# A decode block with attention and a channel MLP: the first load in two transfers, one group's query weights moved, rows of x and biases in nine transfers

## The chip, the cores and the metric

The kernel runs on one core of a Trainium2 chip. The metric is the device time of one execution in microseconds, as the median of three runs. A profiled execution gives a trace: what each engine did and when, what it waited for, and what the 16 DMA engines of the core moved. The engines are TensorE (PE, with its weight loads as PEld), VectorE (DVE), ScalarE (ACT), GpSimd (POOL) and SyncE (SP), which here only issues transfers.

## What is computed

One decode step for 4 tokens of width 448: a layer norm, attention over the last 1024 positions of a cache with 8 groups of 2 query heads of width 256, a residual, then two layer norms and an MLP of width 1792 with a second residual. All is in float32.

```
W = min(4096, max(256, Sk // 4))                      # 1024
q = (x @ wq).reshape(B, Sq, Hq, Dh).transpose(0, 2, 1, 3)
k = jnp.repeat(k_cache[:, :, Sk - W:, :], rep, axis=1)
v = jnp.repeat(v_cache[:, :, Sk - W:, :], rep, axis=1)
p = _softmax(jnp.einsum("bhqd,bhkd->bhqk", q, k) * Dh ** -0.5)
o = jnp.einsum("bhqk,bhkd->bhqd", p, v)               # then reshaped, @ wo
...
h = x + _A_ref(_layernorm(x), A_k_cache, A_v_cache, A_wq, A_wo)
y = _layernorm(_layernorm(h))
h2 = h + (_gelu(y @ w1 + b1) @ w2 + b2)
```

## The kernel before

Every weight and every key and value is used once, so the kernel is a stream of loads into SBUF with work behind it. The host packs the arrays so that one transfer brings what is used next, 128 rows (partitions) at a time.

**Loads.** The tile pool `ring` has three slots of 15872 columns. A load fills a slot whole or in part: `t0` (query weights and x of group 0, keys of group 0, most of the query weights of group 1), then `ta`, `tb`, `tc`, `td` for groups 0 to 2 and again for groups 3 to 5, then three slots `te` with the keys, values and output weights of the last groups and the two MLP matrices w1 and w2. SP issues all of these in the order of the program on one queue. From the fourth load on it waits until the slot's previous content has been read. `load` (L51 on, its transfers at L57) issues one transfer, or several of given widths.

**The opening** (L259 on). `wq0` holds 1792 columns of query weights and 16 columns of x, 128 rows, one transfer of 904 KB. `k0` holds 8192 columns of keys and 1536 columns of the query weights of group 1. Of these weights the last 64 of 448 input rows are missing: they come in `wq1_last`, a tile of 64 rows and 512 columns, by two transfers (L265) of 32 rows each, read from an array whose outer dimension is 8.

**A group's work.** `project_q` (L149) multiplies the normed x (`yT`) with the query weights, four parts side by side in a PSUM tile `pq`; ACT copies it, TensorE transposes it, DVE folds it into `qT`. In `wq_parts` (L69) the fourth part has 64 input rows: packed weights have its two halves of 256 columns one above the other in 128 rows, so it is two matmuls of 256 columns; for group 1 it is one of 512 columns from `wq1_last`. `scores` (L172), `softmax` (L188), `transpose_p` (L204), `values` (L216), `transposed_output` and `add_output` (L245) follow, one group interleaved with the next.

**Rows.** `rs` holds x, b2 and b1 laid out by quadrant: four rows each at partitions 0, 32, 64 and 96, with 128 + 128 + 448 columns. ACT issues these transfers, two a quadrant: 256 columns and 448 columns. Quadrants 0 and 1 go while `tb0` is in use (L302), quadrants 2 and 3 while `td0` is (L319).

**The end** (L324 on). The last group, two layer norms, the MLP (`pu` L437, `pa` L463, `py` L473) and the store at L480. Small matmuls on zeros (`keep_warm`, L345) fill TensorE between its steps.

**The order.** The order of instructions on TensorE, SP and ACT is that of the program; DVE and POOL are ordered by the scheduler.

Of the kernel before, what the change touches and what calls it, by code (L numbers as in the profile page):

```python
# [8 lines left out]
F32 = mybir.dt.float32  # L9
# [6 lines left out]
B, D = 4, 448  # L16
HQ, HKV, SK, DH = 16, 8, 4096, 256
# [3 lines left out]
P = 128  # L21
H = P // 2
ND = 4
NKC = W // P
NFC = F // P
FQ = F // 4
Q = 32
CACHE = NKC * B * DH
HALF = CACHE // 2
WEIGHTS = 4 * D  # L30
# [2 lines left out]
SCALE = DH ** -0.5  # L33

@with_exitstack
def block_kernel(ctx: ExitStack, tc, rows, wq0, k0, wq1, la, lb, lc, ld, k7, vo, w1, w2, out):
    nc = tc.nc
    const = ctx.enter_context(tc.tile_pool(name="const", bufs=1))
    ring = ctx.enter_context(tc.tile_pool(name="ring", bufs=3))
# [10 lines left out]
    def slot(name):  # L50
        return ring.tile([P, SLOT], F32, tag="r", name=name)  # L51

    def load(t, at, src, pieces=None):
        dst = t[:, at : at + src.shape[-1]]
        at = 0
        for n in pieces or (src.shape[-1],):
            nc.sync.dma_start(dst[:, at : at + n], src[:, at : at + n])  # L57
            at += n
        return dst

    def cut(t, sizes):
        parts, at = [], 0
        for n in sizes:
            parts.append(t[:, at : at + n])
            at += n
        return parts


    def wq_parts(t, last=None):  # L69
        parts = [(a, yT[:, a, :], slice(0, 512), t[:, a * 512 : (a + 1) * 512]) for a in range(3)]  # L70
        if last is not None:
            return parts + [(3, yT[:H, 3, :], slice(0, 512), last)]
        for i in range(2):
            parts.append((3, yT[:, 3 + i, :], slice(i * 2 * P, (i + 1) * 2 * P), t[:, 3 * 512 :]))
        return parts


    def keys(t):
        return t.rearrange("p (c b k) -> p c b k", c=2, b=B)

    def chunks(t):
        v = t.rearrange("p (c b d) -> p c b d", b=B, d=DH)
        return [v[:, c : c + 2] for c in range(0, v.shape[1], 2)]
# [17 lines left out]

    yT = const.tile([P, ND + 1, Q], F32, name="yT")
    nc.vector.memset(yT, 0.0)
    wq1_last = const.tile([H, 512], F32, name="wq1_last")
    zT = const.tile([P, ND, Q], F32, name="zT")
    nc.vector.memset(zT, 0.0)

# [41 lines left out]
    def project_q(g, parts):  # L149
        pq = ps_m.tile([P, 512], F32, tag="m", name=f"pq{g}")  # L150
        for j, y, cols, w in parts:
            nc.tensor.matmul(pq[j * Q : (j + 1) * Q, cols], y, w, start=True, stop=True)  # L152
        qs = work.tile([P, 512], F32, tag="qs", name=f"qs{g}")
        nc.scalar.copy(qs, pq)  # L154

        pt = ps_m.tile([P, 2 * REP, P], F32, tag="m", name=f"pqt{g}")
        for i in range(2 * REP):
            nc.tensor.transpose(pt[:, i, :], qs[:, i * P : (i + 1) * P], ident)  # L158
        sm = work.tile([P, 2 * REP, B], F32, tag="sm", name=f"sm{g}")
        nc.vector.tensor_reduce(  # L160
            sm, pt.rearrange("p i (j q) -> p i q j", j=4)[:, :, :B, :], axis=AX.X, op=ALU.add
        )

        src = sm.rearrange("p (r c) b -> p c b r", r=REP)
        for i in range(2):
            nc.vector.tensor_copy(qT[g % 2][:, :, :, i * REP : (i + 1) * REP], src)
# [13 lines left out]
    def softmax(g, parts):  # L180
        halves, mx = zip(*parts)
        nm = work.tile([P, 1], F32, tag="nm", name=f"nm{g}")
        nc.vector.tensor_max(nm, mx[0], mx[1])
        nc.vector.tensor_scalar_mul(nm, nm, -SCALE)  # L184
        p = once.tile([P, 2 * 512], F32, tag="p", name=f"p{g}")
        sums = work.tile([P, 2], F32, tag="sums", name=f"sums{g}")
        for h in range(2):
            nc.scalar.activation(  # L188
                p[:, h * 512 : (h + 1) * 512], halves[h], AF.Exp, bias=nm, scale=SCALE,
                accum_out=sums[:, h : h + 1],  # L190
            )
        rec = work.tile([P, 1], F32, tag=f"rec{g % 3}", name=f"rec{g}")
        nc.vector.tensor_add(rec, sums[:, 0:1], sums[:, 1:2])
        nc.vector.reciprocal(rec, rec)
        return p, rec

    def scores(g, kt):
        return [scores_half(g, h, kt[h]) for h in range(2)]

    def transpose_p(g, p):  # L200
        for h in range(2):
            pt = ps_t.tile([P, 4, P], F32, tag="t", name=f"ppt{g}_{h}")
            for c in range(4):
                nc.tensor.transpose(pt[:, c, :], p[:, (4 * h + c) * P : (4 * h + c + 1) * P], ident)  # L204

            src = pt.rearrange("p (c i) (b q) -> p c i b q", i=2, b=B)
            for i in range(2):
                nc.vector.tensor_copy(
                    pT[g % 2][:, 2 * h : 2 * h + 2, :, i * REP : (i + 1) * REP], src[:, :, i, :, :REP]
                )  # L210


    def values(g, vt, po, pairs=range(NKC // 2)):
        for c in pairs:
            for b in range(B):
                nc.tensor.matmul(  # L216
                    po[b * Q : (b + 1) * Q], pT[g % 2][:, c, b, :], vt[c][:, :, b, :],
                    start=(c == 0), stop=(c == NKC // 2 - 1),
                )
# [35 lines left out]
    def po_tile(g, pool=ps_o, tag="o"):  # L255
        return pool.tile([P, 2, DH], F32, tag=tag, name=f"po{g}")


    t = slot("t0")  # L259
    wqt, xT = cut(load(t, 0, wq0), (WEIGHTS, ND * B))  # L260
    wqt = wq_parts(wqt)
    xT = xT.rearrange("p (a b) -> p a b", a=ND)
    ka, kb, wqt1 = cut(load(t, WEIGHTS + ND * B, k0), (HALF, HALF, 3 * 512))
    for i in range(2):
        nc.sync.dma_start(  # L265
            wq1_last[i * Q : (i + 1) * Q, :], wq1[i].rearrange("e (p c) -> e p c", c=512)[:, :4, :]
        )
    d = work.tile([P, ND, B], F32, tag="d", name="d_x")
    centred(d, xT, "x")
    sx = work.tile([P, ND, B], F32, tag="sx", name="sx")  # L270
# [6 lines left out]
    project_q(0, wqt)  # L277

    parts = scores(0, [keys(ka), keys(kb)])
    project_q(1, wq_parts(wqt1, wq1_last))  # L280
    p, rec = softmax(0, parts)
    transpose_p(0, p)

    def finish(g, po, rec, wt):
        transposed_output(g, po, rec)
        add_output(g, output_weights(wt))

    for g in (0, 3):
        ka, kb, wqt, va = cut(load(slot(f"ta{g}"), 0, la[g // 3]), (HALF, HALF, WEIGHTS, HALF))
        parts = scores(g + 1, [keys(ka), keys(kb)])  # L290
        project_q(g + 2, wq_parts(wqt))
        p, rec_next = softmax(g + 1, parts)
        transpose_p(g + 1, p)
        po = po_tile(g)
        va = chunks(va)
        values(g, va, po, range(0, 2))

        vb, wot, ka, kb = cut(load(slot(f"tb{g}"), 0, lb[g // 3]), (HALF, WEIGHTS, HALF, HALF))
        if g == 0:
            for j in range(2):  # L300
                for cols in (slice(0, 2 * P), slice(2 * P, 2 * P + FQ)):
                    nc.scalar.dma_start(rs[j * Q : j * Q + B, cols], rows[j][:, cols])  # L302
        values(g, va + chunks(vb), po, range(2, 4))
        p, rec_then = softmax(g + 2, scores(g + 2, [keys(ka), keys(kb)]))
        finish(g, po, rec, wot)
        transpose_p(g + 2, p)

        wqt, v, wot, ka = cut(load(slot(f"tc{g}"), 0, lc[g // 3]), (WEIGHTS, CACHE, WEIGHTS, HALF))
        project_q(g + 3, wq_parts(wqt))
        po = po_tile(g + 1)  # L310
        values(g + 1, chunks(v), po)
        first_half = scores_half(g + 3, 0, keys(ka))
        finish(g + 1, po, rec_next, wot)

        kb, wqt, v, wot = cut(load(slot(f"td{g}"), 0, ld[g // 3]), (HALF, WEIGHTS, CACHE, WEIGHTS))
        if g == 0:
            for j in range(2, 4):
                for cols in (slice(0, 2 * P), slice(2 * P, 2 * P + FQ)):
                    nc.scalar.dma_start(rs[j * Q : j * Q + B, cols], rows[j][:, cols])  # L319
        parts = [first_half, scores_half(g + 3, 1, keys(kb))]  # L320
        project_q(g + 4, wq_parts(wqt))
        p, rec = softmax(g + 3, parts)
        transpose_p(g + 3, p)
        po = po_tile(g + 2)  # L324
        values(g + 2, chunks(v), po)
        finish(g + 2, po, rec_then, wot)
# [3 lines left out]
    e = [slot(f"te{i}") for i in range(3)]  # L330
# [7 lines left out]
    p, rec_last = softmax(g + 1, scores(g + 1, kt))  # L338
# [27 lines left out]
    last = ps_s.tile([P, 512], F32, tag="s", name="last")[:, :P]  # L366
# [66 lines left out]
    for a in (0, 1, 3, 2):  # L433
        m = Q if a == 0 else B
        for j in range(4):
            rows, w = w1_part(a, j)
# [24 lines left out]
    for c in range(first):  # L461
        j, m = c % 4, Q if c < 4 else B
# [90 lines left out]
```

## Time and profile before

| | us |
|---|---|
| median of three runs | 213.9 (213.82 to 213.99) |
| the profiled execution | 213.97 |
| its span | 212.2 |
| TensorE busy / weight loads | 133.4 / 47.1 |
| DVE busy / ACT busy | 38.4 / 21.2 |
| loads, 88.46 MB | 417 GB/s over the span |

The span is the time from the first to the last recorded instruction; the execution's own time is longer by what lies around it. A row of windows gives, for a stretch of the span, the busy time of PE, PEld, DVE, ACT and POOL with the number of instructions, then the granted clock of TensorE, the mean busy share of the 16 DMA engines and the GB/s they moved. A packet that begins in a stretch is counted with it whole, so a short stretch can show a share over 1. A row of the timeline gives start, length, engine, line, operation and tiles, and in brackets the idle time before it with what ended it. Rows of digits or GB/s cut a stretch into 40 equal slices.

### The profile page before, as it was taken

How to read it: one execution, taken by the hardware profiler on the slowest of the kernel's cores; microseconds unless marked ns; L12 is line 12 of the kernel's file. 1: busy time of each engine (PE TensorE's matmuls, PEld its weight loads, DVE VectorE, ACT ScalarE, POOL GpSimd, SP SyncE). 2: the span in 40 equal slices, each digit the busy share in tenths (PEclk: the TensorE clock that was granted, in tenths of full speed). 3: DMA queues.
4: the chain of work that ended last, by engine and by line, in shares of the span. 5: the costliest groups of instructions: out<-in, count | busy, mean ns of one | idle time of the engine just before them, and what ended most of it. 6: DMA issues, size and time to landing. Idle time of an engine off the chain costs nothing.

```text
span 212.2 us, 2296 instructions
## 1 busy us (share of the span) xinstructions
PE 133.4 (63%) x970; PEld 47.1 (22%) x970; DVE 38.4 (18%) x167; ACT 21.2 (10%) x52; POOL 5.6 (3%) x17
## 2 busy tenths in 40 slices
PE   0457815841960597188398088138917879978994
PEld 0322201310220221032123022012202322324432
DVE  1420310410230003022014013100200323122310
ACT  2010300300020100030003002001000302010311
POOL 6100000000000000000000000000000000000200
PEclk9999995995896559579969759855885999999999
DMA  7999898999999999999999999999989999999992
GB/s 292 426 396 534 350 499 361 481 416 467 397 419 482 407 420 420 467 393 457 428 425 467 422 407 482 407 431 407 479 349 463 442 399 424 432 393 439 424 398 77
DMA packets 3321, 88.46 MB, mean 417 GB/s; under 512 B 400, under 2 KB 688, under 8 KB 1392
## 3 DMA queue, kind: packets, MB, share of 16 engines
q1 hardware_dynamic: 3248, 88.29, 97.1%
q8 instruction: 7, 0.11, 0.2%
q10 hardware_dynamic: 64, 0.05, 0.1%
q14 instruction: 2, 0.02, 0.0%
HBM read 88.26 MB, written 0.07 MB: 416 GB/s over the span
## 4 chain that ended last, share of the span: by engine, by line
DMA 78%; PE 16%; SPq 2%; DVE 1%; issue 1%; ACT 1%; ACTq 0%
DMA tb<-lb 23%; DMA ta<-la 21%; DMA td<-ld 20%; DMA te<-w 14%; PE s L172 6%; PE po L216 4%; SPq L57 2%; PE ppt L204 1%; PE acc L245 1%; PE pq L152 1%; PE pa L463 1%; PE py L473 1%; SPq L265 1%; PE pqt L158 1%; ACT qs L154 1%
## 5 line engine op out<-in xcount | busy, mean ns | idle before, releaser
L177 DVE TENSOR_REDUCE mx<-s 128x1 f32<-128x512 f32 x16 | 11.1, 691 | 56.1 <-PE s L172 56.1
L172 PE MATMUL s<-ta,qT 128*32 128x512 f32 x64 | 10.7, 830 | 10.1 <-DMA ta<-la 10.1
L154 ACT COPY qs<-pq 128x512 f32<-128x512 f32 x8 | 4.7, 585 | 116.2 <-PE pq L152 116.2
L188 ACT ACTIVATE p<-s,nm 128x512 f32<-128x512 f32 x16 | 10.9, 688 | 46.4 <-DVE nm L184 46.4
L233 DVE TENSOR_SCALAR o<-po,rec 128x512 f32<-128x512 f32 x8 | 6.0, 750 | 50.5 <-PE po L216 50.5
L216 PE MATMUL po<-tb,pT 128*32 128x512 f32 x32 | 6.9, 1019 | 12.9 <-DMA tb<-lb 12.9
L152 PE MATMUL pq<-tc,yT 128*32 128x512 f32 (+1 forms) x20 | 3.9, 891 | 16.8 <-DMA tc<-lc 16.8
L172 PE MATMUL s<-td,qT 128*32 128x512 f32 x32 | 6.9, 1016 | 10.7 <-DMA td<-ld 10.7
L216 PE MATMUL po<-tc,pT 128*32 128x512 f32 x64 | 11.9, 909 | 0.0
L204 PE MATMUL ppt<-ident,p 128*128 128x128 f32 x64 | 10.5, 287 | 0.7 <-ACT p L188 0.4
L158 PE MATMUL pqt<-ident,qs 128*128 128x128 f32 x32 | 6.6, 340 | 6.0 <-ACT qs L154 6.0
L204 PEld LDWEIGHTS ppt<-ident,p 128*128 128x128 f32 x64 | 6.7, 141 | 6.3 <-ACT p L188 6.3
L160 DVE TENSOR_REDUCE sm<-pqt 128x16 f32<-128x64 f32 x8 | 1.8, 224 | 34.4 <-PE pqt L158 34.4
L216 PE MATMUL po<-te,pT 128*32 128x512 f32 x64 | 7.5, 595 | 0.6 <-DMA te<-vo 0.6
L172 PE MATMUL s<-tb,qT 128*32 128x512 f32 x64 | 7.4, 601 | 0.0
L216 PE MATMUL po<-td,pT 128*32 128x512 f32 x64 | 7.3, 595 | 0.0
L237 PE MATMUL pot<-ident,o 128*128 128x128 f32 x32 | 5.3, 287 | 2.7 <-DVE o L233 2.7
L345 PE MATMUL warm<-idle 128*32 128x512 bf16 x22 | 6.8, 382 | 0.0
L158 PEld LDWEIGHTS pqt<-ident,qs 128*128 128x128 f32 x32 | 4.2, 169 | 11.4 <-ACT qs L154 9.7
L172 PE MATMUL s<-t,qT 128*32 128x512 f32 x32 | 5.3, 829 | 2.0 <-DMA t<-k 2.0
L172 PEld LDWEIGHTS s<-ta,qT 128*32 128x32 f32 x64 | 2.6, 147 | 17.5 <-issue 13.5
L146 POOL TENSOR_TENSOR r<-ve_r,mhalf 128x1 f32<-128x1 f32 x2 | 1.1, 542 | 190.3 <-DVE ve_r L145 190.3
(129 smaller groups left out, 112.1 us busy)
## 6 DMA issues: line engine op xcount, KB each, us to landing
tc<-lc SPq DMA_DIRECT2D x2, 7936.0 KB
td<-ld SPq DMA_DIRECT2D x2, 7936.0 KB
ta<-la SPq DMA_DIRECT2D x2, 7040.0 KB
tb<-lb SPq DMA_DIRECT2D x2, 7040.0 KB
te<-vo SPq DMA_DIRECT2D x1, 4992.0 KB
t<-k SPq DMA_DIRECT2D x1, 4864.0 KB
te<-k SPq DMA_DIRECT2D x1, 4096.0 KB
te<-vo SPq DMA_DIRECT2D x1, 3072.0 KB
```

The costliest lines, as they stand in the source:

```text
L57: nc.sync.dma_start(dst[:, at : at + n], src[:, at : at + n])
L152: nc.tensor.matmul(pq[j * Q : (j + 1) * Q, cols], y, w, start=True, stop=True)
L154: nc.scalar.copy(qs, pq)
L158: nc.tensor.transpose(pt[:, i, :], qs[:, i * P : (i + 1) * P], ident)
L172: nc.tensor.matmul(s[b * Q : (b + 1) * Q, :], qT[g % 2][:, c, b, :], kt[:, c, b, :], start=(c == 0), stop=(c == 1),)
L177: nc.vector.reduce_max(m, s, axis=AX.X)
L188: nc.scalar.activation(p[:, h * 512 : (h + 1) * 512], halves[h], AF.Exp, bias=nm, scale=SCALE, accum_out=sums[:, h : h + 1],)
L204: nc.tensor.transpose(pt[:, c, :], p[:, (4 * h + c) * P : (4 * h + c + 1) * P], ident)
L216: nc.tensor.matmul(po[b * Q : (b + 1) * Q], pT[g % 2][:, c, b, :], vt[c][:, :, b, :], start=(c == 0), stop=(c == NKC // 2 - 1),)
L233: nc.vector.tensor_scalar_mul(o, po, rec)
L237: nc.tensor.transpose(pt[:, i, c], o[:, i, c * P : (c + 1) * P], ident)
L345: nc.tensor.matmul(warm[:Q], idle[:, :Q], idle, start=True, stop=True)
```

## The change

Three edits. The array `wq0` is loaded by two transfers, rows 0 to 31 and rows 32 to 127, in place of one. The query weights of group 1 are packed whole behind the keys of group 0, so that `k0` has 9984 columns and not 9728; the tile `wq1_last` with its two transfers and the array `wq1` go, and group 1 uses the same two matmuls of 256 columns as the others. In quadrant 3 the rows of x and of b2 come as two transfers of 128 columns in place of one of 256.

```
-    def wq_parts(t, last=None):
+    def wq_parts(t):
         parts = [(a, yT[:, a, :], slice(0, 512), t[:, a * 512 : (a + 1) * 512]) for a in range(3)]
-        if last is not None:
-            return parts + [(3, yT[:H, 3, :], slice(0, 512), last)]
         for i in range(2):
             parts.append((3, yT[:, 3 + i, :], slice(i * 2 * P, (i + 1) * 2 * P), t[:, 3 * 512 :]))
...
-    wq1_last = const.tile([H, 512], F32, name="wq1_last")
...
     t = slot("t0")
-    wqt, xT = cut(load(t, 0, wq0), (WEIGHTS, ND * B))
+    for p in (slice(0, 32), slice(32, P)):
+        nc.sync.dma_start(t[p, : WEIGHTS + ND * B], wq0[p])
+    wqt, xT = cut(t[:, : WEIGHTS + ND * B], (WEIGHTS, ND * B))
...
-    ka, kb, wqt1 = cut(load(t, WEIGHTS + ND * B, k0), (HALF, HALF, 3 * 512))
-    for i in range(2):
-        nc.sync.dma_start(
-            wq1_last[i * Q : (i + 1) * Q, :], wq1[i].rearrange("e (p c) -> e p c", c=512)[:, :4, :]
-        )
+    ka, kb, wqt1 = cut(load(t, WEIGHTS + ND * B, k0), (HALF, HALF, WEIGHTS))
...
-    project_q(1, wq_parts(wqt1, wq1_last))
+    project_q(1, wq_parts(wqt1))
...
             for j in range(2, 4):
-                for cols in (slice(0, 2 * P), slice(2 * P, 2 * P + FQ)):
+                for cols in ((slice(0, 2 * P), slice(2 * P, 2 * P + FQ)) if j < 3 else (slice(0, P), slice(P, 2 * P), slice(2 * P, 2 * P + FQ))):
                     nc.scalar.dma_start(rs[j * Q : j * Q + B, cols], rows[j][:, cols])
...
-    k0 = np.concatenate([k[0], wq[1][:, : 3 * 512]], axis=1)
-    wq1 = np.asarray(A_wq).reshape(D, HKV, 512)[3 * P :, 1].reshape(2, 8, 4 * 512)
-    wq1 = np.concatenate([wq1, np.zeros((2, 8, 512), np.float32)], axis=2)
+    k0 = np.concatenate([k[0], wq[1]], axis=1)
```

SP's queue at the start of the program, before (a row: line, operation, destination and source with shape; a tile's running number stands behind its name):

```order
L57 DMA t_130<-wq 128x1808
L57 DMA t_130<-k 128x9728
L265 DMA wq_last<-wq 32x1x512 x2
L57 DMA ta_235<-la 128x14080
L57 DMA tb_309<-lb 128x14080
```

and now:

```order
L258 DMA t_129<-wq 32x1808
L258 DMA t_129<-wq 96x1808
L57 DMA t_129<-k 128x9984
L57 DMA ta_234<-la 128x14080
L57 DMA tb_308<-lb 128x14080
```

Two transfers stand ahead of the keys where one stood, and none between the keys and `ta`.

TensorE around the query projection of group 1, before:

```order
L172 MATMUL s_1_184<-t_130,qT_111 32x512 x8
L152 MATMUL pq_195<-t_130,yT 32x512 x3
L152 MATMUL pq_195<-wq_last,yT 32x512
L158 MATMUL pqt_202<-ident,qs_200 128x128 x4
L204 MATMUL ppt_0_221<-ident,p_214 128x128 x4
```

and now:

```order
L169 MATMUL s_1_182<-t_129,qT_110 32x512 x8
L149 MATMUL pq_193<-t_129,yT 32x512 x3
L149 MATMUL pq_193<-t_129,yT 32x256 x2
L155 MATMUL pqt_201<-ident,qs_199 128x128 x4
L201 MATMUL ppt_0_220<-ident,p_213 128x128 x4
```

The place in the queue is the same; the fourth part is two matmuls that read the slot, not one that reads `wq1_last`.

ACT's queue with the rows of quadrants 2 and 3, before:

```order
L154 COPY qs_390<-pq_384 128x512
L319 DMA rs<-rows 4x256
L319 DMA rs<-rows 4x448
L319 DMA rs<-rows 4x256
L319 DMA rs<-rows 4x448
L154 COPY qs_465<-pq_459 128x512
```

and now:

```order
L151 COPY qs_389<-pq_383 128x512
L314 DMA rs<-rows 4x256
L314 DMA rs<-rows 4x448
L314 DMA rs<-rows 4x128 x2
L314 DMA rs<-rows 4x448
L151 COPY qs_465<-pq_459 128x512
```

One transfer of quadrant 3 became two; the work on either side kept its place.

More of the change, by code (lines that the diff above doesn't have):

```diff
@@ L35, in block_kernel @@
 @with_exitstack
-def block_kernel(ctx: ExitStack, tc, rows, wq0, k0, wq1, la, lb, lc, ld, k7, vo, w1, w2, out):
+def block_kernel(ctx: ExitStack, tc, rows, wq0, k0, la, lb, lc, ld, k7, vo, w1, w2, out):
     nc = tc.nc
@@ L537 @@
     arrays = {
-        "rows": rows, "wq0": np.concatenate([wq[0], xT], axis=1), "k0": k0, "wq1": wq1, "la": la, "lb": lb, "lc": lc, "ld": ld, "k7": k[7], "vo": vo, "w1": w1, "w2": w2,
+        "rows": rows, "wq0": np.concatenate([wq[0], xT], axis=1), "k0": k0, "la": la, "lb": lb, "lc": lc, "ld": ld, "k7": k[7], "vo": vo, "w1": w1, "w2": w2,
     }
```

## The prediction

> **What bounds the kernel now.** The page first: the row of the DMA engines, the counts under it, and the queues.
>
> ```profile
> DMA  7999898999999999999999999999989999999992
> DMA packets 3321, 88.46 MB, mean 417 GB/s; under 512 B 400, under 2 KB 688, under 8 KB 1392
> q1 hardware_dynamic: 3248, 88.29, 97.1%
> q8 instruction: 7, 0.11, 0.2%
> q10 hardware_dynamic: 64, 0.05, 0.1%
> ```
>
> All slices but the first and the last are full: the loads are the bound, and only the opening, the share of each of the 16 engines and the tail can move the time. 88.29 MB in 97.1% of 16 x 212.2 us is 26.8 GB/s for an engine. Queue 10 carries the eight small transfers of x and biases: 32 data packets of four rows each, so the other 32 of its 64 must be one completion packet for each engine that took part, four a transfer. By that count the 400 packets under 512 B are 22 full transfers x 16 = 352, these 32, and 16 for the two pieces of wq_last: eight engines each. So today **one half of the engines carries wq_last, 16.4 KB an engine, and the other half nothing**.
>
> Then the end: the chain of waits in order of time, and the last engines in windows (columns: window, length, busy time of five engines, clock, DMA share, GB/s).
>
> ```profile
> 176.52 29.10 DMA te<-w
> 205.76 1.71 PE pa L463 x16
> 209.46 0.29 DVE res L479
> ...
> 206.50:207.00 0.50, 0.50 (x12) 0.13 (x4) 0.00 (x0) 0.00 (x0) 0.00 (x0) 1.00 0.85 333
> 207.00:207.50 0.50, 0.50 (x16) 0.17 (x12) 0.00 (x0) 0.00 (x0) 0.00 (x0) 1.00 0.70 276
> 207.50:208.00 0.50, 0.50 (x24) 0.39 (x16) 0.00 (x0) 0.42 (x1) 0.00 (x0) 1.00 0.57 219
> 208.00:208.50 0.50, 0.50 (x19) 0.24 (x16) 0.00 (x0) 0.11 (x1) 0.00 (x0) 1.00 0.23 86
> 208.50:209.00 0.50, 0.50 (x23) 0.26 (x21) 0.00 (x0) 0.00 (x0) 0.00 (x0) 1.00 0.00 0
> ```
>
> The engines do not stop together. The share falls over some 1.7 us, and the last matmuls wait for the last to stop. The mean does not count; the latest of sixteen does. Part of the spread is made by the seven instruction packets of queue 8: 0.2% of 3395 engine-us is about 1 us for each, and seven such delays cannot fall evenly on sixteen engines.
>
> How hard the tail hangs on the loads, from the timeline (in brackets: the idle time before, and who ended it):
>
> ```profile
> 189.16 1.06 PE L216 MATMUL po<-te,pT 128*32 128x512 f32 x8 [0.20 <-DMA te<-vo]
> 205.76 1.71 PE L463 MATMUL pa<-te,gT 128*32 128x448 f32 x16 [0.24 <-DMA te<-w]
> 208.98 0.11 PEld L473 LDWEIGHTS py<-te,gT 128*4 128x4 f32 x8 [0.24 <-DMA te<-w]
> ```
>
> Three waits of 0.20 to 0.24 us. If the loads come later, the end comes as much later; if they come earlier, TensorE has about 0.2 us to give at each place and then sets the end itself. So a loss passes in full, a gain is capped near 0.2 to 0.4 us.
>
> **The first load**, part one of the change. The opening, in slices of 0.04 us from 1.6 us, and one steady window after it:
>
> ```profile
> GB/s 0 0 0 542 542 181 362 0 0 0 362 0 0 0 0 0 0 0 0 0 0 181 181 542 181 542 362 181 542 0 181 181 904 0 181 723 542 181 181 904
> DMA packets 48, 0.35 MB, mean 217 GB/s; under 512 B 0, under 2 KB 0, under 8 KB 48
> ...
> 3.10:4.30 1.20, 0.00 (x0) 0.00 (x0) 0.00 (x0) 0.00 (x0) 0.94 (x2) 1.00 1.01 428
> 5.57 0.57 PE L131 MATMUL pm_x<-t,mean 128*128 128x12 f32 x2 [5.57 <-DMA t<-wq]
> ```
>
> A packet here is a row of 7232 B, 181 GB/s for one slice. Nine packets begin by 1.88 us (3, 3, 1, 2), two more at 2.0, then none until 2.4: nearly half of the engines open some 0.7 us after the others, and the first packets are slow (eleven begun in 0.7 us, against 0.27 us for one packet at 428/16 = 26.8 GB/s). With two transfers every engine has two rows in the first and six in the second, one completion packet more, about 0.02 us (a small packet of queue 10 takes 0.1% of 3395 us / 64, some 0.05 us, data included). The bytes are the same. What the opening then costs, no row shows; its bounds are these. Below: the late engines open with the others and gain what they were late, 0.7 us less the slow first packet that the early ones have, so at most -0.45 us. Above: if 16 engines cannot write into 32 rows at the rate at which they write into 128, the first part's two packets take double (+0.54 us), and the second part, 64 of whose 96 rows lie in one half of the partitions, takes eight packet times for six (+0.54): +1.08 us. I take **+0.27 us**: the row nearest to it is the opening's own, 217 GB/s, half of the steady 428, so a packet there costs 0.27 us more than a steady one, and I count one such packet for the opening of the second transfer.
>
> The Trainium skill, page "SBUF — State Buffer", section "Door 1: The DMA port swizzle", speaks against the split: partitions 0 to 31 reach only eight of the sixteen ports that DMA writes through, about 218 GB/s. By that figure alone the first part of 231 KB would take an estimated 1.06 us. No row of this trace has all 16 engines writing into 32 partitions, so it neither agrees nor differs yet.
>
> SP's side of it is free:
>
> ```profile
> 0.73 0.38 SPq L57 DMA_DIRECT2D t<-wq  x1
> 1.17 0.41 SPq L57 DMA_DIRECT2D t<-k  x1
> 1.62 1.55 SPq L265 DMA_DIRECT2D wq_last<-wq  x2
> 3.21 0.46 SPq L57 DMA_DIRECT2D ta<-la  x1
> 23.45 0.33 SPq L57 DMA_DIRECT2D tc<-lc  x1
> ```
>
> One issue of 0.4 us is added ahead of the keys, and 1.55 us are removed behind them. The keys are issued at 1.6 instead of 1.17 us; their first byte is needed when the first load ends, some 4.4 us. Then ta comes earlier. Cover: the first load itself.
>
> **The query weights**, part two. Two transfers of 64 KB go, 128 x 256 columns x 4 B = 131 KB are added to the keys' rows. Each of the eight loses 16.4 KB / 26.8 = 0.61 us, all sixteen gain 8.2 KB, 0.31 us. Net: **-0.31 us on one half, +0.31 us on the other**. The sum over engines is unchanged; the latest engine decides. Which half ends last no view tells: bounds -0.31 and +0.31. I take +0.31, because both halves should have an engine among the last unless the seven instruction packets all fell on one of them, and then the half that gains decides.
>
> On TensorE the last quarter of group 1 is two matmuls of 256 columns over 128 rows, not one of 512 over 64:
>
> ```profile
> 22.36 1.05 PE L152 MATMUL pq<-t,yT 128*32 128x512 f32 x6
> 23.33 1.04 PE L152 MATMUL pq<-wq_last,yT 64*32 64x512 f32 x2
> 17.30:50.00 32.70, 19.20 (x122) 6.47 (x121) 5.74 (x26) 3.87 (x10) 0.00 (x0) 0.86 1.01 436
> ```
>
> The columns streamed are the same and it is done by 24.4 us; behind it on TensorE stand the transposes and then group 1's scores, which wait for ta, at 33 us. The slot t0 is released by all five matmuls instead of three, so tc's issue, at 23.45 us, moves back up to 1 us. The DMA engines have ta and tb queued (share 1.01 until 50 us). Price nothing; without that cover, 1 us.
>
> **The rows in nine transfers**, part three. The x and b2 of quadrant 3 go as two transfers of 512 B a row. One issue more on ACT:
>
> ```profile
> 72.79 1.29 ACTq L319 DMA_DIRECT2D rs<-rows  x4
> ACT qs L154 <- PE pq L152: 116.2, 8, 20.8
> ```
>
> 0.3 us on a queue whose next work waits for td, for up to 20.8 us: nothing. On the DMA side two packets more, 0.05 us each, on four engines: +0.1 us there at most, taken at 0 on the end, since with +0.31 on the other half these four need not be last. No wait is added on SP that another load does not cover.
>
> **Sum**: +0.27 + 0.31 + 0.02 = +0.60 us. The profiled execution took 213.97 us, its span 212.2 and 1.8 around it; its median is 0.07 lower, 213.9. So **214.5 us**. 0.2%, 0.43 us, is about what a measurement of this kernel can tell from no change.
>
> **Rivals.** *The late engines open with the others.* For it: the gap from 2.1 to 2.4 us, and a first transfer with a quarter of the rows. Against it: the first packets are slow on the early engines too, which a shorter transfer does not mend. Then the half that gains 0.31 us is the one that no longer starts late: +0.31 + 0.02 - 0.45 = -0.12, to -0.4 where everything opens earlier and the tail's cap allows it: 213.8, 213.5 at best.
>
> *Engines meet at the same rows.* Pairs of engines write into the same few partitions while the 32 rows go, and two thirds of the 96 rows into one half. It decides as soon as the pace at a group of partitions is that of one engine, 0.27 us a row: +1.08 + 0.31 + 0.02 = +1.4 at the full price, 215.3; at two thirds 214.95, which I take. Against it: the opening is slow anyway and hides some. This is how the rule of the Trainium skill quoted above ("SBUF — State Buffer", "Door 1") would work here.
>
> *Nothing reaches the end.* The engines that instruction packets delayed are last in both, and all in the half that loses 0.31 us, which pays for the opening: 213.9.
>
> **Numbers.** Forecast 0.35 (own range 214.1 to 214.8), engines meeting 0.28, late engines cured 0.27, nothing 0.10. Slower: 0.28, all but 0.08 of the forecast, and 0.01: 0.56. Faster than 0.2%: half of the cured case, 0.14. Within: 0.30. The range takes in the cured case's best and the full price of meeting: 213.5 to 215.4.
>
> **What would show it.** Right: 400 + 16 - 16 + 4 = 404 packets under 512 B; the last of the first load's packets not before 5 us; the first packets of ta spread wider than before; the share at 208.5 to 209.0 no longer 0. Meeting: packets of 7232 B that take 0.5 us in 2.5 to 5 us. Cured: sixteen packets begun by 2.1 us. The prediction is wrong if the opening costs nothing, or if the engines that end last are those that carried wq_last.

## The result, and the profile after

| | before | changed |
|---|---|---|
| median, us | 213.87 (213.78 to 213.99, 6 runs) | 214.94 (214.90 to 214.99, 6 runs) |
| the profiled execution / its span | 213.97 / 212.2 | 214.92 / 213.1 |
| ratio to before, 95% interval | | 1.0047 (1.0037 to 1.0058) |

The change costs 1.07 us, 0.5%, with an interval that excludes no change: slower, inside the range, and nearly twice the +0.60 us of the forecast. The page of the changed kernel, its DMA rows (q1 is the queue of SP, q10 that of ACT):

```profile
DMA packets 3265, 88.46 MB, mean 415 GB/s; under 512 B 404, under 2 KB 696, under 8 KB 1336
q1 hardware_dynamic: 3184, 88.29, 97.2%
```

The bytes are the same and the share of busy time is too (97.2 against 97.1%). The 404 small packets are those counted ahead: 16 more for the second part, 16 fewer for wq_last, 4 more for the ninth transfer. So the engines were as busy and moved less in a microsecond. Where they did so is seen at the opening: the GB/s in slices of 0.04 us from 1.6 us with the stretch's packet count, then the packets of 3.3 to 5.1 us with their share of the 16 engines, then TensorE's first matmul.

```profile
GB/s 0 0 0 181 723 181 542 181 362 0 181 181 0 0 0 0 0 181 0 181 542 542 0 542 723 0 362 362 724 181 181 723 362 181 0 181 181 0 0 0
DMA packets 64, 0.35 MB, mean 217 GB/s; under 512 B 16, under 2 KB 16, under 8 KB 64
...
DMA packets 69, 0.50 MB, mean 277 GB/s; under 512 B 0, under 2 KB 0, under 8 KB 69
q1 hardware_dynamic: 69, 0.50, 103.5%
...
6.72 0.57 PE L128 MATMUL pm_x<-t,mean 128*128 128x12 f32 x2 [6.72 <-DMA t<-wq]
```

Before, from 3.2 to 4.3 us:

```profile
DMA packets 64, 0.46 MB, mean 421 GB/s; under 512 B 0, under 2 KB 0, under 8 KB 64
q1 hardware_dynamic: 64, 0.46, 99.7%
```

Three readings. Fourteen packets begin by 2.08 us (1, 4, 1, 3, 1, 2, 1, 1), against eleven before. That is a small difference: five of the experiments below leave the first load undivided, and their profiles have nine to twelve by 2.1 us. By 3.2 us both kernels have begun 48 rows (here 64 packets less the 16 small ones), so up to there the split costs nothing. But from 3.3 us on the 69 packets of one row each take 103.5% of 16 x 1.8 us, 0.43 us apiece, where a row took 0.27 before (99.7% of 16 x 1.1 us for 64). As a mean over the 16 engines there is no idle time; the packets are slow. x arrives 1.15 us later (6.72 against 5.57 us).

The end, in windows of the same length, each 1 us later than those shown of the kernel before:

```profile
207.50:208.00 0.50, 0.50 (x12) 0.13 (x4) 0.00 (x0) 0.00 (x0) 0.00 (x0) 1.00 0.88 344
208.00:208.50 0.50, 0.50 (x16) 0.16 (x12) 0.00 (x0) 0.00 (x0) 0.00 (x0) 1.00 0.75 298
208.50:209.00 0.50, 0.50 (x24) 0.41 (x16) 0.00 (x0) 0.40 (x1) 0.00 (x0) 1.00 0.62 237
209.00:209.50 0.50, 0.50 (x18) 0.19 (x16) 0.00 (x0) 0.13 (x1) 0.00 (x0) 1.00 0.34 129
209.50:210.00 0.50, 0.50 (x24) 0.32 (x24) 0.00 (x0) 0.00 (x0) 0.00 (x0) 1.00 0.00 0
```

The fall from 0.85 to 0 is the one of before, 1 us later. What was lost at the opening is carried through 200 us of full queues to the end almost whole: 1.15 us there, 1.0 us here. And the tail hangs on the loads as it did:

```profile
190.18 1.06 PE L213 MATMUL po<-te,pT 128*32 128x512 f32 x8 [0.22 <-DMA te<-vo]
206.77 1.71 PE L458 MATMUL pa<-te,gT 128*32 128x448 f32 x16 [0.23 <-DMA te<-w]
210.45 0.29 DVE res L474
```

Each step stands 1.0 us later than before (189.16, 205.76, 209.46) with the same short waits for a load.

### The profile page after: what moved, and what is told of

It reads as the page before. It is cut to its first block, busy times and chain, and to the rows that moved or that the text cites. A ratio compares the mean times of both kernels' runs of the same rounds, so it can differ in the third digit from the quotient of the medians.

```text
span 213.1 us, 2300 instructions
## 1 busy us (share of the span) xinstructions
PE 133.5 (63%) x972; PEld 47.4 (22%) x972; DVE 38.1 (18%) x167; ACT 21.2 (10%) x52; POOL 5.6 (3%) x17
## 3 DMA queue, kind: packets, MB, share of 16 engines
q1 hardware_dynamic: 3184, 88.29, 97.2%
## 4 chain that ended last, share of the span: by engine, by line
DMA 70%; PE 21%; another core or an unknown queue 3%; SPq 2%; DVE 1%; ACT 1%; issue 1%; ACTq 0%
DMA ta<-la 36%; DMA td<-ld 20%; DMA te<-w 14%; PE s L169 9%; PE po L213 5%; PE ppt L201 2%; PE pq L149 1%; SPq L57 1%; PE acc L242 1%; PE pqt L155 1%; ACT qs L151 1%; PE pa L458 1%; PE py L468 1%; SPq L258 0%
## 5 line engine op out<-in xcount | busy, mean ns | idle before, releaser
L213 PE MATMUL po<-tc,pT 128*32 128x512 f32 x64 | 11.4, 879 | 0.0
L169 PE MATMUL s<-tb,qT 128*32 128x512 f32 x64 | 8.4, 673 | 0.0
```

Source lines behind the costliest of these rows:

```text
L169: nc.tensor.matmul(s[b * Q : (b + 1) * Q, :], qT[g % 2][:, c, b, :], kt[:, c, b, :], start=(c == 0), stop=(c == 1),)
L213: nc.tensor.matmul(po[b * Q : (b + 1) * Q], pT[g % 2][:, c, b, :], vt[c][:, :, b, :], start=(c == 0), stop=(c == NKC // 2 - 1),)
```

## The experiments

**Which of the three edits.** Each alone, against the kernel before.

The split alone:

```
-    wqt, xT = cut(load(t, 0, wq0), (WEIGHTS, ND * B))
+    for p in (slice(0, 32), slice(32, P)):
+        nc.sync.dma_start(t[p, : WEIGHTS + ND * B], wq0[p])
```

> The kernel before with the first load in two transfers of 32 and 96 rows, nothing else changed. If the price of the change is in writing into part of the rows: the first load ends some 0.65 us later on every engine, the half that still carries wq_last is last, and the time is about 214.65 (213.9 + 0.8). If the split is free and the price is in the moved weights: 213.9. If the late half of the engines is cured by it and nothing is paid: 213.8 or less.

Measured 215.37 us, ratio 1.0068 (1.0056 to 1.0081): +1.47 us, more than the whole change. The weights are not the price.

The weights alone (`k0` with the whole `wq[1]`, no `wq1_last`):

> The kernel before with group 1's query weights whole behind the first keys, one first load, eight transfers of rows. If this part costs what its bytes take on the half of the engines that carried nothing (+0.31 us): 214.15. If it is the price of the whole change: 214.9. If the half that loses bytes is the one that ends last: 213.6 to 213.9.

Measured 214.06 us, 1.0006 (0.9997 to 1.0015): +0.16 us, which the interval does not tell from none, and well below 214.9.

The ninth transfer alone (the change's line for quadrant 3):

> The kernel before with x and b2 of quadrant 3 in two transfers. Two more small packets on four engines: 213.9, at most 0.1 us more. If small transfers delay the queue of loads by whole packets: 0.5 us or more, 214.4.

Measured 214.01 us, 1.0005 (0.9997 to 1.0014): +0.11 us, not told from none; half a microsecond is excluded.

**Two transfers, or parts of the rows?** The changed kernel with the first load divided the other way:

```
-    for p in (slice(0, 32), slice(32, P)):
-        nc.sync.dma_start(t[p, : WEIGHTS + ND * B], wq0[p])
+    load(t, 0, wq0, (904, 904))
```

> The changed kernel with the first load split by columns, two transfers of 904 columns over all 128 rows, in place of 32 and 96 rows. If the price lies in which rows a transfer writes: it is gone, and the time is that of moved weights alone, 214.15. If any second transfer at the opening costs it: 214.9 as with the change.

Measured 213.97 us, 1.0007 (0.9998 to 1.0017). It has the moved weights, the ninth transfer and a second transfer at the opening; only the rows are whole. So by the medians 214.94 - 213.97 = 0.97 us of the 1.07 is the division by rows (0.86 us by the two ratios). Its opening, in GB/s (window 3.2 to 4.4 us), over that of the changed kernel:

```profile
3.20:4.40 1.20, 0.00 (x0) 0.00 (x0) 0.00 (x0) 0.00 (x0) 0.83 (x2) 1.00 1.16 473
```

```profile
3.20:4.40 1.20, 0.00 (x0) 0.00 (x0) 0.00 (x0) 0.00 (x0) 0.84 (x2) 1.00 1.11 319
```

Equal busy shares, 473 against 319 GB/s.

**Which rows.** Two halves, then the same number of rows taken alternately, both in the changed kernel:

```
-    for p in (slice(0, 32), slice(32, P)):
+    for p in (slice(0, 64), slice(64, P)):                 # halves
+    for p in (slice(0, P, 2), slice(1, P, 2)):             # even and odd
```

> The changed kernel with the first load in rows 0 to 63 and 64 to 127. If the engines meet at the doors of the rows (half of the partitions takes half of the full rate): eight packet times of 0.27 us become sixteen, +2.16 us on an undivided first load at 214.0: about 216.1. If a part of the rows has a fixed price at the opening, or the small first part is what costs: 214.9 or less, as with 32 and 96.

> The changed kernel with the first load in even rows and odd rows, 64 each over all partitions. If the price hangs on which partitions a transfer covers: gone, 214.0 or a little less if all engines open together. If it hangs on the number of rows, whichever they are, because engines no longer keep to their own rows: like halves of 64 rows, 215 to 216.1.

Halves: 215.83 us, 1.0090 (1.0075 to 1.0105), 1.86 us over the column parts. Some 0.3 us of this is a later start: SP needs longer for the two issues (first the changed kernel, then the halves), and the first packet begins at 2.04 us in place of 1.72.

```profile
0.74 0.85 SPq L258 DMA_DIRECT2D t<-wq  x2
0.73 1.19 SPq L258 DMA_DIRECT2D t<-wq  x2
```

The other 1.5 us compare with the 2.16 of a load at half the rate. Even and odd: a median of 215.33, with five runs between 214.24 and 215.71, four of them at 215.05 or more. The profiled execution was the one of 214.24, and it ran at the full rate:

```profile
3.20:4.40 1.20, 0.00 (x0) 0.00 (x0) 0.00 (x0) 0.00 (x0) 0.85 (x2) 1.00 1.04 217
```

```profile
3.20:4.40 1.20, 0.00 (x0) 0.00 (x0) 0.00 (x0) 0.00 (x0) 0.83 (x2) 1.00 1.05 434
```

First the halves, then even and odd: 217 against 434 GB/s at the same share, with 64 rows to a transfer in both. So it is not the number of rows. Even and odd rows can run at the full rate; what slowed the four other executions no trace shows, and for the small first load the question stays open.

**A price of the opening, or of the bytes?** The first load whole, and the second, 39.9 KB a row, divided in three ways:

```
+    at = WEIGHTS + ND * B
+    for p in (slice(0, 32), slice(32, P)):                 # or even and odd
+        nc.sync.dma_start(t[p, at : at + CACHE + WEIGHTS], k0[p])
...
+    load(t, WEIGHTS + ND * B, k0, (4992, 4992))            # columns
```

> The changed kernel with the first load whole and the second (keys of group 0 and query weights of group 1, 39.9 KB a row against 7.2) in 32 and 96 rows. If the price goes with the bytes: 5.5 times the 0.97 us of the first load, +5.3 us on 214.0, about 219.3. If it is a price of the opening or of a second transfer: 214.0 to 214.9.

> The changed kernel with the first load whole and the second in even and odd rows instead of 32 and 96. If the rate hangs on which partitions a transfer covers, a transfer over all of them runs near the full rate even with half of the rows: 214 to 216. If every transfer of fewer than 128 rows runs at half the rate: 226.5, as with 32 and 96 rows.

> The changed kernel with the first load whole and the second in two transfers of 4992 columns over all rows. If a second transfer as such costs nothing: 214.0. If dividing the large load costs whatever the direction: several us more, towards 226.5.

Rows 0 to 31 and 32 to 127: 226.50 us, 1.0588 (1.0572 to 1.0604). Even and odd: 214.06, 1.0009 (0.9999 to 1.0018). Columns: 214.16, 1.0013 (1.0004 to 1.0022). The stretches from 6 to 16 and from 16 to 26 us, first of the 32 and 96 rows, then of even and odd:

```profile
6.00:16.00 10.00, 5.23 (x22) 3.30 (x22) 3.26 (x20) 0.58 (x1) 1.03 (x1) 1.00 0.91 192
16.00:26.00 10.00, 0.00 (x0) 0.00 (x0) 0.39 (x3) 0.00 (x0) 0.00 (x0) 1.00 1.15 252
```

```profile
6.00:16.00 10.00, 0.71 (x3) 0.59 (x3) 2.07 (x12) 0.00 (x0) 0.00 (x0) 1.00 1.00 431
16.00:26.00 10.00, 4.62 (x22) 2.50 (x26) 1.57 (x10) 0.59 (x1) 1.03 (x1) 1.00 1.04 451
```

The price grows with the bytes and belongs to no opening. The same load, 5.1 MB, the same number of transfers and fewer than 128 rows in a transfer in both: the 32 and 96 rows move 192 and 252 GB/s in the two stretches; the even and odd rows move 431 in the first, and the second already holds the load behind them. What differs is which rows a transfer covers. A row of the array always goes to the partition of the same number here, so no run tells whether the engines meet where they write or where they read; and halves of 64 neighbouring rows were not tried for this load.

My expectation for 32 and 96 rows, 219.3 us, was too low: +12.3 us over the columns is as much again as the whole load takes (5.1 MB at 428 GB/s, 11.9 us), so the 96 rows ran at half the rate as well. The trace shows it: from 12 to 27 us, all within the 96 rows, 80 packets take 98.9% of 16 x 15 us, 3.0 us each, where 39.9 KB at 26.8 GB/s take 1.5.

**Both halves at once?** Rows 0 to 63 by SP, rows 64 to 127 by ACT:

```
+    for q, p in ((nc.sync, slice(0, 64)), (nc.scalar, slice(64, P))):
+        q.dma_start(t[p, : WEIGHTS + ND * B], wq0[p])
```

> The changed kernel with rows 0 to 63 of the first load issued by SP and rows 64 to 127 by ACT at the same time. If engines meet at the doors of one half only while the other half stands behind it: both halves are open at once, the price is gone, 214.0. If it is in how 64 rows are dealt to 16 engines: as with the two halves from one queue, 215 to 216.1.

Measured 215.80 us, 1.0086 (1.0071 to 1.0101), as with one queue. But it did not test what it was meant to, as the queues from 1.8 to 3.4 us and from 3.9 to 5.5 us show:

```profile
q1 hardware_dynamic: 56, 0.40, 92.3%
```

```profile
q10 hardware_dynamic: 48, 0.35, 97.1%
q1 hardware_dynamic: 8, 0.00, 0.7%
```

Both were issued at 0.73 to 0.74 us, and yet in the first stretch only SP's queue moved, and in the second only ACT's moved rows (the eight packets of SP's carry 0.00 MB): the halves went one after the other.

**A better version?** The column parts' opening on the kernel before (wq_last kept):

> The kernel before with the first load in two transfers of 904 columns, all else as before. The opening with two column parts ended 0.1 us earlier in one profile (4.96 against 5.08 us): if that reaches the end, 213.8, better than both kernels; if it is noise or hidden, 213.9. It cannot show the row price: nothing here covers a part of the rows.

Measured 214.30 us (214.01 to 215.43), 1.0024 (1.0012 to 1.0036). This is 0.4 us slower than the kernel before; why some of its runs are so long was not followed. So two column parts are not free everywhere: 213.97 us without wq_last, 214.30 with it. No version tried beats the kernel before.

## Why the prediction came out as it did

**The bound** was right: the loads set the end, and a loss at the opening reaches it nearly in full. The cap on a gain, TensorE's 0.2 us at each wait, was not put to the test, as nothing was gained.

**The first load** is where the sum failed. I took +0.27 us between -0.45 and +1.08, as a slow packet of a second opening; it is 0.97 (the changed kernel against column parts). A second opening alone is not the price: the column parts open twice too, in 213.97 us. The cause is the division by rows, as in the rival *engines meet at the same rows*, which I gave 0.28; its sign, packets of 0.5 us, nearly came with 0.43. Shown is that the rate hangs on which rows a transfer covers; the meeting of the engines itself no view shows. So the direction was right and the time lay in the range, but outside the likeliest case's own 214.1 to 214.8, and that case had the wrong cause and a term at a quarter of its size.

That the rival's 214.95 meets the 214.94 measured is partly luck. It counted 0.72 for the rows (two thirds of 1.08) and 0.33 for the rest; measured are 0.97 and about 0.1. Its working, +0.54 for each part, does not hold either. The 32 rows paid nothing beyond what the slow opening cost before, as the 48 rows by 3.2 us show; the rival allowed that the opening hides some. The 96 rows paid all, by an estimate from the packets: 0.16 us more for each of the five or six rows that an engine still had, 0.8 to 1.0 us. That is 1.6 packet times for one, where I reckoned eight for six; with the long rows it is two for one. The point from which the rival was to decide, half of the rate as soon as the engines share a group of partitions, holds for halves: 217 GB/s.

The Trainium skill, "SBUF — State Buffer", section "Door 1: The DMA port swizzle", puts partitions 0 to 31, and 0 to 63, at no more than about 218 GB/s. The trace agrees with 217 for halves. By the port map in that section of the Trainium skill the even rows reach all sixteen ports. The trace agrees with 431 GB/s for even and odd rows of the large load. By the same map of the Trainium skill rows 32 to 127 reach all sixteen ports too. The section of the Trainium skill gives no half rate for them; there the measurement stands alone.

**The late engines.** That the split cures them, as the second rival said, is not shown. Its sign was sixteen packets by 2.1 us, and fourteen came. What is measured is that wq_last costs more once the first load comes in two transfers. Divided by rows: 215.37 us with it, 214.94 without. By columns: 214.30 with it, 213.97 without. With an undivided load moving its weights costs 0.16 (214.06 against 213.90), not told from none. (The two without it have the ninth transfer as well, whose +0.11 is not told from none.) As the columns show it too, it does not hang on the rows. The reading that wq_last filled the engines that opened late, and burdens one half once all open together, fits but is argued: no view labels the engines, and the count of small packets gives eight engines for each piece of wq_last, not the same eight for both.

**The signs.** Those of the forecast came, with one exception: 404 small packets, rows of the first load beginning after 5 us, a share of 0.62 at 208.5 to 209.0 us. But the first packets of ta were to spread wider, and they stand closer together. GB/s in slices of 0.055 us from 16.0 us, before and now; 1024 is one packet of ta:

```profile
GB/s 112 186 2123 261 261 74 1285 1285 75 1285 2309 112 3221 3109 2048 1024 0 0 0 0 0 0 0 0 0 0 0 0 0 0 0 0 0 0 0 0 0 0 0 1024
GB/s 726 3631 2904 726 1452 0 0 0 0 0 0 0 0 0 0 0 0 0 0 0 0 0 0 0 0 1024 2048 1024 5120 4096 2048 1024 0 0 0 0 0 0 0 0
```

Before, the sixteen begin within about 0.7 us, between packets of wq_last; now within about 0.35 us.

**The query weights**: +0.31 forecast, +0.16 measured on its own, not told from none; with the load divided by rows the move gains 0.4. The term depends on the opening, and I treated it as independent. **The rows**: 0 forecast, +0.11, not told from none. **TensorE, SP and ACT**: free as said.

```profile
24.31 0.33 SPq L57 DMA_DIRECT2D tc<-lc  x1
73.83 1.64 ACTq L314 DMA_DIRECT2D rs<-rows  x5
```

tc is issued 0.86 us later (23.45 before) under loads that run to 50 us, and ACT's issues take 0.35 us more while it waits.

## What to carry to other kernels

If a load must be divided, divide it by columns, not into blocks of neighbouring rows: against the kernel before, two column parts over all 128 partitions cost 0.1 us (with the moved weights) or 0.4 us (without) for a load of 0.9 MB and 0.3 us for one of 5.1 MB, while 32 and 96 rows cost 12.3 us more there. A busy DMA share says nothing about the rate: look at GB/s beside it, stage by stage, and at the time of one packet of known size. A term measured alone need not hold beside another edit: moving wq_last's weights cost 0.16 us alone and gained 0.4 us beside the split, so such edits are to be costed together.

## What was not expected of the hardware

- Rows 32 to 127, 16 engines, 39.9 KB a row: 3.0 us a packet, half of the full rate, though they reach into both halves of the partitions. How 96 rows are dealt to the engines no run here settles.
- Even and odd rows: 213.94 to 214.31 us in ten runs with the large load, but 214.24 to 215.71 in five with the small first one.
- Two transfers issued at the same time by SP and ACT went one after the other, not side by side (56 packets of one queue, then 48 of the other).
